# Wider weight conversion and a seven-product scheme for block 0's second product, with w_out's sums on VectorE

## The chip, the cores and the metric

The kernel runs on one core of a Trainium2 chip. The metric is device time in microseconds (us). "Span" is the time from the first to the last instruction of the profiled execution; it is some 2 us shorter than the time.

## The reference, cut to what matters

```python
for t in range(S):                       # B=4, H=8, S=768, D=64
    state = gamma * state + k[t] (outer) v[t]
    y[t] = scale * q[t] @ state
x = y as (3072 tokens, 512)
h = x @ w_in                             # 512 x 2048
g = h * sigmoid(1.702 * h)
out = g @ w_out                          # 2048 x 512
```

The weights come as 64-bit floats and are narrowed to 32-bit ones on the chip, with integer operations on the halves of each number.

## The kernel before

The tokens go in six blocks of 512 (m = 0 to 5), each of four chunks of 128 (24 chunks, j). Per chunk, `turn` transposes q and k, `attend` multiplies k and q and applies a mask, and `finish` gives x and the next state. Then come two products per block, "up" (x @ w_in, with a gate) and "down" (gated @ w_out). Blocks 2 to 5 use a seven-product scheme (Strassen-Winograd) for both; block 1 for the second; block 0 for none, since the sums of weight blocks that the scheme needs aren't there yet.

While TensorE does the plain up-products, VectorE and ScalarE convert the weights, one piece of 512 numbers per partition at a time:

```python
def narrow(n=1):
    ...
        act.activation(m, hi, AF.Abs, scale=2.0 ** 16)
        dve.tensor_scalar(m, m, MOST, LEAST, op0=min, op1=max)
        dve.tensor_scalar(mu, mu, 3, None, op0=logical_shift_left)
        dve.scalar_tensor_tensor(hi, hi, 0x80000000, mu, op0=and, op1=or)
        dve.tensor_scalar(mu, hi, 0xFF800000, None, op0=and)
        dve.scalar_tensor_tensor(r, lo, 2.0 ** -52, m, op0=mult, op1=mult)
        dve.tensor_add(w, hi_f, lo_f)
        fetch()                                    # the next piece
...
load(0); fetch(); load(1)                          # q, k, v of chunks 0 and 1
for _ in range(NRAW - 1): fetch()                  # NRAW = 4 pieces ahead
turn(0)                                            # issues chunk 2's q and k
for j in range(CB):                                # the head
    attend(j); narrow(1); turn(j + 1); finish(j); narrow(1)
    if j: up0(0, j - 1)
...
for f in range(NFF): up1(f); narrow(1)             # block 1's up-product
for f in range(NFF):                               # block 0's second product, 64 x 512 columns
    down0(f)
    if f % 4 == 3: sums_w2(f // 2 - 1)             # w_out's sums, on GpSimd
for m in range(1, NB): ...                         # blocks 1 to 5
```

Of the kernel before, what the change touches and what calls it, by code (L numbers as in the profile page):

```python
# [9 lines left out]
F32 = mybir.dt.float32  # L10
# [3 lines left out]
P = 128  # L14
# [14 lines left out]
def kernel(  # L29
# [64 lines left out]
    G0 = one.tile([P, 2, TH], F32, name="g0", tag="s1")  # L94
# [10 lines left out]
    def load(j, what="qkv"):  # L105
# [13 lines left out]
        else:  # L119
            for name, src in (("q", q), ("k", k)):  # L120
                t = two.tile([P, HP, P // C4, C4], F32, name=name + "_sq")
                for r0 in range(0, P, C4):
                    d0 = r0 % D
                    for hp in range(HP):
                        sp.dma_start(t[r0:r0 + C4, hp],
                                     src[b, 2 * hp + r0 // D, rows, d0:d0 + C4].rearrange("(s p) d -> p s d", p=C4))
                QKV[name, j] = t
            if c < NC - 1:
                plain("kn", k, "kn", 1)
        if "v" in what:  # L130
# [5 lines left out]
    NRAW = 4  # L136
    RAWS = [W2[:, 4 + i // 2, i % 2 * 4:i % 2 * 4 + 4].rearrange("p n e -> p (n e)").bitcast(U32)
            .rearrange("p (n two) -> p n two", two=2) for i in range(NRAW)]


    PIECES = []
    for p in range(NP):
        for h in range(2):
            dst = W1[:, p, 0:4:3] if h == 0 else W1[:, p, 1:3]
            PIECES.append((dst.rearrange("p ab c f -> p c ab f"), w1v[:, 2 * h:2 * h + 2, 2 * p * P:2 * (p + 1) * P],
                           dst.rearrange("p ab c f -> p ab (c f)")))
    for p in range(NP):
        for ab in range(2):
            dst = W2[:, 0:4:3, p] if ab == 0 else W2[:, 1:3, p]
            PIECES.append((dst, w2v[:, 2 * p + ab], dst))  # L150
    N1 = 2 * NP
    fetched = [0]

    def fetch():
        i = fetched[0]
        if i < len(PIECES):
            x = RAWS[i % NRAW]
            src = PIECES[i][1]
            sp.dma_start(x.rearrange("p (c f) two -> p c f two", c=2) if i < N1 else x, src)
            fetched[0] = i + 1  # L160
# [3 lines left out]
    def narrow(n=1):  # L164


        for _ in range(n):
            i = narrowed[0]
            if i == len(PIECES):
                return  # L170
            narrowed[0] = i + 1
            (w, _, m), x = PIECES[i], RAWS[i % NRAW]
            mu = m.bitcast(U32)
            two_runs = x.rearrange("p (a b) two -> p a b two", a=2)
            lo, hi = two_runs[:, :, :, 0], two_runs[:, :, :, 1]

            tc.keep_in_program_order(act.activation(m, hi.bitcast(F32), AF.Abs, scale=2.0 ** 16))
            tc.keep_in_program_order(dve.tensor_scalar(m, m, F64_MOST * 2.0 ** 16, F64_LEAST * 2.0 ** 16,  # L178
                                                       op0=ALU.min, op1=ALU.max))
            dve.tensor_scalar(mu, mu, 3, None, op0=ALU.logical_shift_left)  # L180
            dve.scalar_tensor_tensor(hi, hi, 0x80000000, mu, op0=ALU.bitwise_and, op1=ALU.bitwise_or)  # L181
            dve.tensor_scalar(mu, hi, 0xFF800000, None, op0=ALU.bitwise_and)  # L182
            r = lo.bitcast(F32)
            dve.scalar_tensor_tensor(r, lo, 2.0 ** -52, m, op0=ALU.mult, op1=ALU.mult)  # L184
            xf = x.bitcast(F32)
            if i < N1:
                xf = xf.rearrange("p (c ab f) two -> p c ab f two", c=2, ab=2)
                dve.tensor_add(w, xf[:, :, :, :, 1], xf[:, :, :, :, 0])
            else:
                xf = xf.rearrange("p (s e) two -> p s e two", s=2)  # L190
# [366 lines left out]
```

## Time and profile before

| | before |
|---|---|
| time, median of 4 | 732.94 us (732.53 to 735.52) |
| span of the profiled execution | 730.7 us |
| first up-product starts | 25.79 us |
| third up-product starts; from here TensorE isn't idle until 171.0 us | 46.99 us |
| block 1's up-product starts | 113.36 us |
| block 0's second product starts | 168.30 us |
| block 1's second product starts | 225.97 us |

The starts are read from TensorE's timeline. A line of a timeline gives the start and duration in us, the engine, the source line, the operation, output and inputs, the shape and the count, and in brackets how long the engine was idle before it and what ended that. The chain view gives start, duration and work only; its pieces start up to 0.17 us later than the timeline's, where two matmuls overlap. The lines of before are in the prediction.

### The profile page before, as it was taken

To read this page: it belongs to the slowest core of one execution; us is meant where nothing else is said; L and a number is where in the kernel's file an instruction comes from. 1 tells how busy PE (TensorE), PEld (TensorE's weight loads), DVE (VectorE), ACT (ScalarE), POOL (GpSimd) and SP (SyncE) were. 2 spreads that over 40 slices of the span, in tenths; PEclk is the share of its full clock that TensorE was granted. 3 is DMA by queue.
4 is the path that set the end of the run, shared out by engine and by line. 5 is a ranking of instruction groups with operands and counts; after the bars stand their busy time and mean duration, and the time that the engine had idled before them with its cause. 6 is when DMAs were issued, how large, how long until landed. Compare 5 with 4: busy or idle time off the path is not lost.

```text
span 730.7 us, 9512 instructions
## 1 busy us (share of the span) xinstructions
PE 710.6 (97%) x3680; PEld 569.1 (78%) x3680; DVE 365.0 (50%) x603; ACT 126.5 (17%) x209; POOL 137.9 (19%) x127
## 2 busy tenths in 40 slices
PE   5799999998999999999999999999999999999997
PEld 4678885443447888888888888888888888888886
DVE  4999977994002643442653344464344272244251
ACT  3322313330000000332000233000233000133000
POOL 3231010028533223000233100022200140200030
PEclk9999999999999999999999999999999999999999
DMA  9876454530001324300334310234300210100001
GB/s 244 212 179 172 119 125 100 157 123 1 0 0 59 73 47 85 71 1 1 66 56 89 61 21 1 49 57 88 74 10 0 49 39 1 44 1 0 15 0 44
DMA packets 142252, 46.26 MB, mean 63 GB/s; under 512 B 129920, under 2 KB 135552, under 8 KB 142208
## 3 DMA queue, kind: packets, MB, share of 16 engines
q1 hardware_dynamic: 135504, 39.10, 24.1%
q10 hardware_dynamic: 6704, 6.57, 2.7%
q8 instruction: 29, 0.48, 0.3%
q14 instruction: 15, 0.12, 0.1%
HBM read 39.33 MB, written 6.29 MB: 62 GB/s over the span
## 4 chain that ended last, share of the span: by engine, by line
PE 85%; DVE 13%; DMA 1%; issue 1%; SPq 0%; ACT 0%
PE pd L408 32%; PE px L357 15%; PE py L357 11%; PE po L317 7%; PE ph L292 7%; PE py L249 3%; PE pa L232 3%; PE pu L262 3%; PE py L245 2%; DVE W L184 2%; DVE W L181 2%; DVE W L191 1%; DVE G L279 1%; DVE W L178 1%; DVE W L182 1%; DMA q_in<-in_q_dram 1%
## 5 line engine op out<-in xcount | busy, mean ns | idle before, releaser
L408 PE MATMUL pd<-W,G 128*128 128x256 f32 x1120 | 250.3, 381 | 0.4 <-DVE G L348 0.3
L408 PEld LDWEIGHTS pd<-W,G 128*128 128x128 f32 x1120 | 210.1, 190 | 31.2 <-DVE G L348 1.2
L357 PE MATMUL px<-X,W 128*128 128x256 f32 x512 | 119.0, 379 | 0.0
L357 PEld LDWEIGHTS px<-X,W 128*128 128x128 f32 x512 | 97.3, 190 | 13.2
L357 PE MATMUL py<-X,W 128*128 128x256 f32 x384 | 90.7, 379 | 0.0
L357 PEld LDWEIGHTS py<-X,W 128*128 128x128 f32 x384 | 73.0, 190 | 9.9
L292 PE MATMUL ph<-X,W 128*128 128x256 f32 x256 | 58.2, 382 | 2.2 <-DVE X L253 2.2
L223 POOL TENSOR_TENSOR kd<-kn_in,cold 128x512 f32<-128x512 f32 x13 | 14.9, 1147 | 240.0 <-DMA q_sq<-in_q_dram 126.5
L305 PE MATMUL ph<-W,W 128*128 128x512 f32 x128 | 55.1, 592 | 0.0
L292 PEld LDWEIGHTS ph<-X,W 128*128 128x128 f32 x256 | 47.5, 190 | 8.9 <-DVE X L253 2.4
L349 POOL TENSOR_TENSOR G<-G 128x512 f32<-128x512 f32 x20 | 28.9, 1443 | 111.6 <-DVE G L348 107.0
L235 DVE TENSOR_TENSOR at<-pa,mask 128x512 f32<-128x512 f32 x32 | 20.6, 684 | 58.7 <-PE pa L232 58.7
L305 PEld LDWEIGHTS ph<-W,W 128*128 128x128 f32 x128 | 24.3, 190 | 30.2 <-issue 29.4
L317 PE MATMUL po<-W,W 128*128 128x512 f32 x96 | 42.8, 593 | 2.5 <-DVE G L279 2.5
L279 DVE TENSOR_TENSOR G<-G,sg 128x512 f32<-128x512 f32 x48 | 33.0, 688 | 13.8 <-ACT sg L277 13.8
L277 ACT ACTIVATE sg<-G 128x512 f32<-128x512 f32 x48 | 30.3, 631 | 51.0 <-DVE G L367 30.7
L317 PEld LDWEIGHTS po<-W,W 128*128 128x128 f32 x96 | 18.2, 190 | 25.8 <-issue 22.0
L277 ACT ACTIVATE sg<-ph 128x512 f32<-128x512 f32 x32 | 19.1, 598 | 105.0 <-PE ph L292 44.0
L269 POOL TENSOR_TENSOR state<-state,cold 64x256 f32<-64x256 f32 x32 | 23.2, 725 | 46.4 <-DVE state L267 23.1
L367 DVE TENSOR_TENSOR G<-py,p 128x512 f32<-128x512 f32 x16 | 11.1, 692 | 37.8 <-PE py L357 37.8
L320 DVE COPY o<-po 128x512 f32<-128x512 f32 x4 | 2.8, 692 | 51.8 <-PE po L317 50.3
L395 ACT ACTIVATE u<-pd 128x512 f32<-128x512 f32 x5 | 3.0, 597 | 134.1 <-PE pd L408 134.1
(87 smaller groups left out, 696.7 us busy)
## 6 DMA issues: line engine op xcount, KB each, us to landing
W<-in_moe_w_in_dram SPq DMA_DIRECT2D x16, 512.0 KB, 3.8
W<-in_moe_w_out_dram SPq DMA_DIRECT2D x16, 512.0 KB, 3.5
v_in<-in_v_dram SPq DMA_DIRECT2D x24, 256.0 KB, 4.0
out_dram<-o ACTq DMA_DIRECT2D x24, 256.0 KB, 2.3
kn_in<-in_k_dram SPq DMA_DIRECT2D x21, 256.0 KB, 3.6
q_sq<-in_q_dram SPq DMA_DIRECT2D x256, 16.0 KB, 1.9
k_sq<-in_k_dram SPq DMA_DIRECT2D x256, 16.0 KB, 1.8
q_in<-in_q_dram SPq DMA_DIRECT2D x8, 256.0 KB, 4.6
```

The source lines that it names most:

```text
L232: pe.matmul(p[:, i, hp, :], KT[j][r, hp, :], QT[j][r, hp, :], start=True, stop=True)
L249: pe.matmul(y[i * D:(i + 1) * D, hp, :], vn[:, 2 * hp + i, :], a[:, i, hp, :], start=(not c and hp == 0), stop=(hp == HP - 1), skip_group_ ...
L262: pe.matmul(u[:, hp, :], kd[:, h, :].rearrange("p i d -> p (i d)"), vn[:, h, :].rearrange("p i d -> p (i d)"), start=True, stop=True)
L269: pool.tensor_mul(new[r, :, r], old[r, :, r], cold[r, 2 * H:, None].to_broadcast([D, HP, D]))
L277: act.activation(s, h, AF.Sigmoid, scale=1.702)
L279: dve.tensor_mul(g, h[:, i], s[:, i])
L292: pe.matmul(h[:, ab], w, X[:, 2 * half + c // 2, c % 2, :], start=(ab == 0 and c == 0), stop=(c == 3), skip_group_check=True)
L305: pe.matmul(h, w, X1[:, c // 2:4:2, c % 2, :], start=(c == 0), stop=(c == 3))
L317: pe.matmul(PO[n], g0(p, 2 * half + ab)[:, t0:t0 + P], w, start=(f == 0), stop=(f == NFF - 1))
L349: pool.tensor_sub(g[1], g[1], g[0])
L357: pe.matmul(acc[:, u, :], W1[:, 2 * d + u, sa, c, :], X[:, sb, c, :], start=(start and u == 0 and c == 0), stop=(stop and c == 1), skip_gr ...
L408: pe.matmul(p0[:, n, :], G[:, p, sa, n * P:(n + 1) * P], W2[:, sb, p, :], start=(new and p == 0 and n == 0), stop=(last and p == NP - 1), ...
```

## The change

Four things change together. The weights are converted 1024 numbers at a time (all but the first two pieces), which makes half as many VectorE instructions of it. By 512 a tensor_scalar operation steps in 0.34 us and a two-input one in 0.60. There are six raw buffers instead of four, so six pieces are fetched ahead. Block 0's second product uses the seven-product scheme. For that w_out's sums must be ready before it, and they move from GpSimd to VectorE. A fifth thing goes with the first: the calls of the converter stand differently, so that by the program's order 22 of the 32 pieces come before block 1's up-product, where it was 18.

```diff
-    NRAW = 4
+    RAWS = [... for r in (W2[:, 4], W2[:, 5], G[:, 6:8]...)]    # three of 1024, six pieces
 def narrow():
+        n = 1 if i < 2 else 2
...
-    for _ in range(NRAW - 1):
+    for _ in range(5):
         fetch()
...
 for f in range(NFF):
     up1(f)
-    narrow(1)
+    if f % 2 == 0:
+        narrow()
+    if f >= NFF - 4:
+        sums_w2(2 * (f - NFF + 4))            # three sums each, now dve.tensor_sub
-for f in range(NFF):
-    down0(f)
-    if f % 4 == 3:
-        sums_w2(f // 2 - 1)
-for m in range(1, NB):
+for m in range(NB):
...
     for n, unit in enumerate(down(m)):
         unit()
+        if m == 0 and n < NP // 2:
+            sums_w2_t3(2 * n)                 # the fourth sum, dve.tensor_sub
```

(Cut: the operand numbering, where block 0's gated values are kept, and the converter's calls in the head and beside block 0's up-product. The loads of transposed q and k are now kept in program order.)

More of the change, by code (lines that the diff above doesn't have):

```diff
@@ L93 @@
     G = const.tile([P, NP, 4, TH], F32, name="G")
-    G0 = one.tile([P, 2, TH], F32, name="g0", tag="s1")
+    G0 = one.tile([P, 2, TH], F32, name="g0", tag="kd")
     X1 = W2[:, 6].rearrange("p (s c) t -> p s c t", s=4)
@@ L124, in load @@
                     for hp in range(HP):
-                        sp.dma_start(t[r0:r0 + C4, hp],
-                                     src[b, 2 * hp + r0 // D, rows, d0:d0 + C4].rearrange("(s p) d -> p s d", p=C4))
+                        tc.keep_in_program_order(sp.dma_start(
+                            t[r0:r0 + C4, hp],
+                            src[b, 2 * hp + r0 // D, rows, d0:d0 + C4].rearrange("(s p) d -> p s d", p=C4)))
                 QKV[name, j] = t
@@ L135 @@
     w2v = moe_w_out.bitcast(U32).rearrange("(f p) (e two) -> p f e two", p=P, two=2)
-    NRAW = 4
-    RAWS = [W2[:, 4 + i // 2, i % 2 * 4:i % 2 * 4 + 4].rearrange("p n e -> p (n e)").bitcast(U32)
-            .rearrange("p (n two) -> p n two", two=2) for i in range(NRAW)]
-    PIECES = []
-    for p in range(NP):
-        for h in range(2):
-            dst = W1[:, p, 0:4:3] if h == 0 else W1[:, p, 1:3]
-            PIECES.append((dst.rearrange("p ab c f -> p c ab f"), w1v[:, 2 * h:2 * h + 2, 2 * p * P:2 * (p + 1) * P],
-                           dst.rearrange("p ab c f -> p ab (c f)")))
@@ L147, with raw @@
-    for p in range(NP):
-        for ab in range(2):
-            dst = W2[:, 0:4:3, p] if ab == 0 else W2[:, 1:3, p]
-            PIECES.append((dst, w2v[:, 2 * p + ab], dst))
-    N1 = 2 * NP
+    RAWS = [r.rearrange("p a b -> p (a b)").bitcast(U32)
+            for r in (W2[:, 4], W2[:, 5], G[:, 6:8].rearrange("p a s t -> p a (s t)"))]
+    SRC = [w1v[:, 2 * h:2 * h + 2, 2 * p * P:2 * (p + 1) * P] for p in range(NP) for h in range(2)] \
+        + [w2v[:, f] for f in range(NFF)]
     fetched = [0]
+    def raw(i, n=1):
+        x = RAWS[i // 2 % 3]
+        return x[:, i % 2 * 1024:(i % 2 + n) * 1024]
@@ L154, in fetch @@
     def fetch():
         i = fetched[0]
-        if i < len(PIECES):
-            x = RAWS[i % NRAW]
-            src = PIECES[i][1]
-            sp.dma_start(x.rearrange("p (c f) two -> p c f two", c=2) if i < N1 else x, src)
+        if i < len(SRC):
+            x = raw(i).rearrange("p (n two) -> p n two", two=2)
+            sp.dma_start(x.rearrange("p (c f) two -> p c f two", c=2) if i < NFF else x, SRC[i])
             fetched[0] = i + 1
     narrowed = [0]
-    def narrow(n=1):
-        for _ in range(n):
-            i = narrowed[0]
-            if i == len(PIECES):
-                return
-            narrowed[0] = i + 1
-            (w, _, m), x = PIECES[i], RAWS[i % NRAW]
-            mu = m.bitcast(U32)
-            two_runs = x.rearrange("p (a b) two -> p a b two", a=2)
-            lo, hi = two_runs[:, :, :, 0], two_runs[:, :, :, 1]
-            tc.keep_in_program_order(act.activation(m, hi.bitcast(F32), AF.Abs, scale=2.0 ** 16))
-            tc.keep_in_program_order(dve.tensor_scalar(m, m, F64_MOST * 2.0 ** 16, F64_LEAST * 2.0 ** 16,
-                                                       op0=ALU.min, op1=ALU.max))
-            dve.tensor_scalar(mu, mu, 3, None, op0=ALU.logical_shift_left)
-            dve.scalar_tensor_tensor(hi, hi, 0x80000000, mu, op0=ALU.bitwise_and, op1=ALU.bitwise_or)
-            dve.tensor_scalar(mu, hi, 0xFF800000, None, op0=ALU.bitwise_and)
-            r = lo.bitcast(F32)
-            dve.scalar_tensor_tensor(r, lo, 2.0 ** -52, m, op0=ALU.mult, op1=ALU.mult)
-            xf = x.bitcast(F32)
-            if i < N1:
-                xf = xf.rearrange("p (c ab f) two -> p c ab f two", c=2, ab=2)
-                dve.tensor_add(w, xf[:, :, :, :, 1], xf[:, :, :, :, 0])
-            else:
-                xf = xf.rearrange("p (s e) two -> p s e two", s=2)
-                dve.tensor_add(w, xf[:, :, :, 1], xf[:, :, :, 0])
@@ new lines, in narrow @@
+    def narrow():
+        i = narrowed[0]
+        if i == len(SRC):
+            return
+        n = 1 if i < 2 else 2
+        narrowed[0] = i + n
+        p, h = i // 2 % NP, i % 2
+        if i < 2:
+            m = W1[:, 1, 2 * h:2 * h + 2].rearrange("p s c f -> p (s c f)")
+            w = W1[:, 0, h:4:2].rearrange("p ab c f -> p c ab f")
+        elif i < NFF:
+            m = W1[:, p, 0:4].rearrange("p s c f -> p (s c f)")
+            w = W1[:, p, 0:4].rearrange("p (ab h) c f -> p (h c) ab f", ab=2)
+        else:
+            m = w = W2[:, 0:4, p]
+        x = raw(i, n).rearrange("p (n two) -> p n two", two=2)
+        lo, hi = x[:, :, 0], x[:, :, 1]
+        if i >= NFF:
+            lo, hi = [t.rearrange("p (s e) -> p s e", s=4) for t in (lo, hi)]
+        mu = m.bitcast(U32)
+        tc.keep_in_program_order(act.activation(m, hi.bitcast(F32), AF.Abs, scale=2.0 ** 16))
+        tc.keep_in_program_order(dve.tensor_scalar(m, m, F64_MOST * 2.0 ** 16, F64_LEAST * 2.0 ** 16,
+                                                   op0=ALU.min, op1=ALU.max))
+        dve.tensor_scalar(mu, mu, 3, None, op0=ALU.logical_shift_left)
+        dve.scalar_tensor_tensor(hi, hi, 0x80000000, mu, op0=ALU.bitwise_and, op1=ALU.bitwise_or)
+        dve.tensor_scalar(mu, hi, 0xFF800000, None, op0=ALU.bitwise_and)
+        dve.scalar_tensor_tensor(lo.bitcast(F32), lo, 2.0 ** -52, m, op0=ALU.mult, op1=ALU.mult)
+        lo, hi = lo.bitcast(F32), hi.bitcast(F32)
+        if i < NFF:
+            lo, hi = [t.rearrange("p (c ab f) -> p c ab f", ab=2, f=P) for t in (lo, hi)]
+        dve.tensor_add(w, hi, lo)
+        for _ in range(n):
@@ L201, in home @@
         if j >= 2 * CB:
-            return one.tile([P] + shape, F32, name=name)
-        t = G[:, j % 2 * 4 + at, 0:2 if at < 3 else 4].rearrange("p s t -> p (s t)")
+            return one.tile([P] + shape, F32, name=name, tag=name)
         if at < 3:
-            return t.rearrange("p (a b) -> p a b", a=shape[0])
-        return t.rearrange("p (a b c) -> p a b c", a=2, b=HP)
+            t = G[:, at, j % 2 * 2:j % 2 * 2 + 2]
+            return t.rearrange("p s t -> p (s t)").rearrange("p (a b) -> p a b", a=shape[0])
+        return G[:, 3 + j % 2].rearrange("p s t -> p (s t)").rearrange("p (a b c) -> p a b c", a=2, b=HP)
     def turn(j):
@@ L218, in turn @@
             else:
-                dve.transpose(t.rearrange("p h t -> p (h t)"), QKV.pop((name, j)).rearrange("p h s d -> p (h s d)"))
+                tc.keep_in_program_order(dve.transpose(
+                    t.rearrange("p h t -> p (h t)"), QKV.pop((name, j)).rearrange("p h s d -> p (h s d)")))
             store[j] = t
@@ L279, in hidden, with g, g1 @@
             dve.tensor_mul(g, h[:, i], s[:, i])
-    def g0(p, s):
+    def g(m, p, s):
+        if m:
+            return G[:, p:p + 2, s, :]
         if s < 3:
-            return W1[:, p, 4 + s].rearrange("p c f -> p (c f)")
-        return X[:, 4 + p // 2, p % 2] if p < 6 else G0[:, p % 2]
+            return W1[:, p:p + 2, 4 + s].rearrange("p a c f -> p a (c f)")
+        return X[:, 4 + p // 2] if p < 6 else G0
+    def g1(m, p, s):
+        return g(m, p // 2 * 2, s)[:, p % 2]
     def up0(half, p):
@@ L290, in up0 @@
             for c in range(4):
-                w = W1[:, p, (c // 2 if ab == 0 else (3, 2)[c // 2]), c % 2, :]
+                w = W1[:, p, 2 * ab + c // 2, c % 2, :]
                 pe.matmul(h[:, ab], w, X[:, 2 * half + c // 2, c % 2, :], start=(ab == 0 and c == 0), stop=(c == 3),
@@ L296, in up0 @@
         else:
-            hidden([(g0(p, 2 + i), i) for i in range(2)], h)
+            hidden([(g1(0, p, 2 + i), i) for i in range(2)], h)
     def up1(f):
@@ L303, in up1 @@
         for c in range(4):
-            w = W1[:, p, (c // 2 if ab == 0 else (3, 2)[c // 2]), c % 2, :]
+            w = W1[:, p, 2 * ab + c // 2, c % 2, :]
             pe.matmul(h, w, X1[:, c // 2:4:2, c % 2, :], start=(c == 0), stop=(c == 3))
         hidden(G[:, p, ab:4:2, :], h)
-    PO = {}
-    def down0(f):
-        p, ab = divmod(f, 2)
-        for n in range(CB):
-            if f == 0:
-                PO[n] = ps.tile([P, 2, EH], F32, name="po", tag="xy"[n % 2])
-            half, t0 = divmod(n * P, TH)
-            w = W2[:, 0:4:3, p, :] if ab == 0 else W2[:, 1:3, p, :]
-            pe.matmul(PO[n], g0(p, 2 * half + ab)[:, t0:t0 + P], w, start=(f == 0), stop=(f == NFF - 1))
-            if f == NFF - 1:
-                o = two.tile([P, 2, EH], F32, name="o")
-                dve.tensor_copy(o, PO[n])
-                act.dma_start(out[n * P:(n + 1) * P, :], o.rearrange("p a e -> p (a e)"))
@@ L324, in sums_w1 @@
     def sums_w1(p):
         w = [W1[:, p:p + 2, s] for s in range(7)]
-        pool.tensor_add(w[4], w[3], w[2])
-        pool.tensor_sub(w[6], w[0], w[3])
+        pool.tensor_add(w[4], w[2], w[3])
+        pool.tensor_sub(w[6], w[0], w[2])
         pool.tensor_sub(w[5], w[4], w[0])
-        pool.tensor_sub(w[3], w[1], w[5])
-    def sums_b(b):
-        pool.tensor_sub(b[4], b[3], b[0])
-        pool.tensor_sub(b[6], b[2], b[3])
-        pool.tensor_sub(b[5], b[2], b[4])
-        pool.tensor_sub(b[3], b[1], b[5])
@@ L338, in sums_w2, with sums_x @@
-    def sums_w2(p):
-        sums_b([W2[:, s, p:p + 2, :] for s in range(7)])
-    def sums_x():
-        sums_b([X[:, s] for s in (0, 1, 3, 2, 4, 5, 6)])
-    def sums_g(p):
-        g = [G[:, p:p + 2, s, :] for s in range(4)]
-        dve.tensor_add(g[3], g[2], g[3])
-        dve.tensor_sub(g[2], g[0], g[2])
-        dve.tensor_sub(g[0], g[3], g[0])
-        pool.tensor_sub(g[1], g[1], g[0])
+        pool.tensor_sub(w[2], w[1], w[5])
+    def sums_x():
+        pool.tensor_sub(X[:, 4], X[:, 2], X[:, 0])
+        pool.tensor_sub(X[:, 6], X[:, 3], X[:, 2])
+        pool.tensor_sub(X[:, 5], X[:, 3], X[:, 4])
+        pool.tensor_sub(X[:, 2], X[:, 1], X[:, 5])
@@ new lines, in sums_w2, with sums_w2_t3, sums_g @@
+    def sums_w2(p):
+        w = [W2[:, s, p:p + 2, :] for s in range(7)]
+        dve.tensor_sub(w[4], w[1], w[0])
+        dve.tensor_sub(w[5], w[3], w[4])
+        dve.tensor_sub(w[1], w[2], w[5])
+    def sums_w2_t3(p):
+        dve.tensor_sub(W2[:, 6, p:p + 2, :], W2[:, 5, p:p + 2, :], W2[:, 0, p:p + 2, :])
+    def sums_g(m, p):
+        a = [g(m, p, s) for s in range(4)]
+        dve.tensor_add(a[3], a[2], a[3])
+        dve.tensor_sub(a[2], a[0], a[2])
+        dve.tensor_sub(a[0], a[3], a[0])
+        pool.tensor_sub(a[1], a[1], a[0])
@@ L358, in product @@
                               start=(start and u == 0 and c == 0), stop=(stop and c == 1), skip_group_check=True)
-        g = [G[:, 2 * d:2 * d + 2, s, :] for s in range(4)]
+        a = [G[:, 2 * d:2 * d + 2, s, :] for s in range(4)]
         x = ps.tile([P, 2, TH], F32, name="px", tag="x")
@@ L366, in up @@
         product(y, 1, 1, True, True)
-        dve.tensor_add(g[0], y, p1)
-        hidden(g[0], g[0])
+        dve.tensor_add(a[0], y, p1)
+        hidden(a[0], a[0])
         product(x, 5, 5, False, False)
@@ L379, in up @@
         y = ps.tile([P, 2, TH], F32, name="py3", tag="y")
-        product(y, 3, 3, True, True)
-        dve.tensor_add(g[3], z, vv)
-        hidden(g[3], g[3])
-        dve.tensor_add(g[2], y, t)
-        hidden(g[2], g[2])
-        product(x, 2, 2, False, True)
-        hidden(g[1], x)
+        product(y, 2, 3, True, True)
+        dve.tensor_add(a[3], z, vv)
+        hidden(a[3], a[3])
+        dve.tensor_add(a[2], y, t)
+        hidden(a[2], a[2])
+        product(x, 3, 2, False, True)
+        hidden(a[1], x)
     def down(m):
@@ L407, in part @@
                 for n in range(2):
-                    pe.matmul(p0[:, n, :], G[:, p, sa, n * P:(n + 1) * P], W2[:, sb, p, :],
+                    pe.matmul(p0[:, n, :], g1(m, p, sa)[:, n * P:(n + 1) * P], W2[:, sb, p, :],
                               start=(new and p == 0 and n == 0), stop=(last and p == NP - 1), skip_group_check=True)
@@ L422, in down @@
         P_ = [("x", 0, 0, True, False, lambda x: keep("p1", "s1", x)),
-              ("y0", 1, 1, True, True, lambda y: put(0, 0, y, kept["p1"])),
-              ("y1", 3, 3, True, True, lambda y: None),
+              ("y0", 1, 2, True, True, lambda y: put(0, 0, y, kept["p1"])),
+              ("y1", 3, 1, True, True, lambda y: None),
               ("x", 0, 5, False, False, lambda x: keep("u", "s2", x)),
@@ L427, in down @@
               ("x", 2, 6, False, True, then_p7),
-              ("x2", 1, 2, True, True, lambda y: put(0, 1, y, kept["t"]))]
+              ("x2", 1, 3, True, True, lambda y: put(0, 1, y, kept["t"]))]
         todo = []
@@ L434, in unit @@
                     if n == 2:
-                        sums_g(2 * d)
+                        sums_g(m, 2 * d)
                 todo.append(unit)
@@ L470 @@
     turn(0)
-    units = [(half, p) for p in range(3, NP) for half in range(2)]
     for j in range(CB):
         attend(j)
-        narrow(1)
+        narrow()
         turn(j + 1)
         finish(j)
-        narrow(1)
-        if j:
+        if j == 0:
+            narrow()
+        else:
             up0(0, j - 1)
     between = chunks(1)[1:]
-    for n, unit in enumerate([(1, p) for p in range(3)] + units):
+    for n, unit in enumerate([(1, p) for p in range(3)] + [(half, p) for p in range(3, NP) for half in range(2)]):
         up0(*unit)
-        if n < NP or n % 2:
-            narrow(1)
+        if n % 2 == 0:
+            narrow()
         if between:
@@ L488 @@
         up1(f)
-        narrow(1)
+        if f % 2 == 0:
+            narrow()
+        if f >= NFF - 4:
+            sums_w2(2 * (f - NFF + 4))
         if f >= NFF - 2:
             load(2 * CB + f - NFF + 2)
-    for f in range(NFF):
-        down0(f)
-        if f % 4 == 3:
-            sums_w2(f // 2 - 1)
-    for m in range(1, NB):
-        between = chunks(m + 1) if m + 1 < NB else []
+    for m in range(NB):
+        between = chunks(m + 1) if 0 < m < NB - 1 else []
         if m > 1:
```

## The prediction

Three passages of the prediction are cut: on VectorE beside GpSimd, on what an instruction costs, and on the rates of two kinds of operation. This case shows only the times beside them. No term of the sum is cut: 732.8 - 8.6 - 0.5 + 0.4 = 724.1 us. The 0.07 us fixed is the author's estimate from the steps of 0.34 and 0.60 us, and the closing 0.34 and 0.60 are the steps of a tensor_scalar and of a two-input operation of 512 numbers. The 10 us of slack in rival 2 is an estimate as well: three buffers beyond the one in use, at 54.8/16 = 3.43 us each.

> **What bounds the kernel now.** I read the page's engine rows first, then the chain that ended last, then that chain in order of time, and last the timelines of the places where the chain leaves TensorE. From the page:
>
> ```profile
> PE 710.6 (97%) x3680; PEld 569.1 (78%) x3680; DVE 365.0 (50%) x603; ACT 126.5 (17%) x209; POOL 137.9 (19%) x127
> PE   5799999998999999999999999999999999999997
> PEld 4678885443447888888888888888888888888886
> DVE  4999977994002643442653344464344272244251
> PE 85%; DVE 13%; DMA 1%; issue 1%; SPq 0%; ACT 0%
> ```
>
> The reader is to see two things. TensorE is busy in every slice after the second, so nearly everything that leaves its stream comes off the time, and nothing else does. VectorE is full only in the first quarter, while the weights are converted. The 13% that the chain gives to VectorE look like a second bound, but TensorE is busy all that while: the chain merely follows one wait back through the converter. The chain in order of time and TensorE's timeline around that wait:
>
> ```profile
> 113.53 3.45 PE ph L305 x8
> ...
> 171.21 1.63 DVE W L191
> 173.50 52.62 PE po L317 x122
> 226.13 6.91 PE pd L408 x32
> ```
> ```profile
> 159.71 8.75 PE L305 MATMUL ph<-W,W 128*128 128x512 f32 x20
> 168.30 2.74 PE L317 MATMUL po<-W,W 128*128 128x512 f32 x6
> 173.50 2.84 PE L317 MATMUL po<-W,W 128*128 128x512 f32 x6 [2.47 <-DVE G L279]
> ```
>
> These give the rates. A 512-wide matmul record takes 52.62/122 = 0.4313 us, a 256-wide one 6.91/32 = 0.2159 us: the same per column, so narrow products cost nothing extra. (The mean durations in the group rows, 593 and 381 ns, overlap and mustn't be added.) The program's matmuls each make two records: 64 of block 0's second product give 96 + 24 + 8 = 128. That product runs from 168.30 to 226.13, 57.83 us: 128 x 0.4313 = 55.21, plus the wait of 2.47.
>
> That wait is the converter's tail, on VectorE's timeline:
>
> ```profile
> 156.36 0.41 DVE L182 TENSOR_SCALAR W<-W 128x512 uint32<-128x512 uint32 x1
> 156.69 0.41 DVE L178 TENSOR_SCALAR W<-W 128x512 f32<-128x512 f32 x1
> 157.03 0.67 DVE L184 SCALAR_TENSOR_TENSOR W<-W 128x512 f32<-128x512 uint32 x1
> ...
> 169.54 1.64 DVE L184 SCALAR_TENSOR_TENSOR W<-W 128x512 f32<-128x512 uint32 x1
> 171.21 1.63 DVE L191 TENSOR_TENSOR W<-W 128x512 f32<-128x512 f32 x1
> 172.77 0.68 DVE L279 TENSOR_TENSOR G<-ph,sg 128x512 f32<-128x512 f32 x1
> ```
>
> VectorE runs back to back, and where GpSimd has begun w_out's sums a 0.68 us operation takes 1.64. The last block-0/1 gate (the multiply at 172.77) is late, it holds a PSUM buffer, and the product starts late.
>
> [...] 0.68 becomes 1.64 beside GpSimd. [...] a 256-wide multiply in a run of independent ones steps in 0.34 us (54.73 to 55.07), a 512-wide one in 0.60, so 0.26 is streaming and about 0.07 fixed. [...] the trace's steps are 0.34 and 0.60.
>
> **The change, part by part.**
> Block 0's product. Removed: 128 records of 512 = 55.21 us, and the wait of 2.47. Added: 7 products x 4 units x 4 matmuls = 112, or 224 records of 256, x 0.2159 = 48.36 us. Exactly seven eighths. This lies wholly on TensorE, on the path. The new product starts on gates finished long before (block 0's) and needs one PSUM buffer that the third-last gate frees, so I take the 2.47 as gone. It brings the wait that every seven-product block has between its third and fourth product, where the operand sums are made. The last block, which like block 0 has no attention work beside it, shows its size:
>
> ```profile
> 677.00 26.41 PE L408 MATMUL pd<-W,G 128*128 128x256 f32 x120
> ...
> 695.03 1.58 POOL L349 TENSOR_TENSOR G<-G 128x512 f32<-128x512 f32 x1 [67.37 <-DVE G L348]
> 695.52 1.64 DVE L347 TENSOR_TENSOR G<-G 128x512 f32<-128x512 f32 x1
> ...
> 703.69 22.71 PE L408 MATMUL pd<-W,G 128*128 128x256 f32 x104 [0.28 <-DVE G L348]
> ```
>
> 120 x 0.2159 = 25.91, so TensorE restarts 703.69 - 677.00 - 25.91 = 0.8 us late. Stage after: 48.36 + 0.8 = 49.2; before 57.8; gain **8.6 us**.
>
> Conversion by 1024. One piece of 512 is three tensor_scalar and three two-input operations: 3 x 0.34 + 3 x 0.60 = 2.8 us where independent work fills the gaps, 3.43 where each waits for the one before (118.24 to 121.67). A pair of 1024, by the fixed 0.07, is 3 x 0.60 + 3 x 1.13 = 5.2, or 5.8 with those waits once instead of twice. Saved per pair 0.4 to 1.05; 15 pairs, 6.5 to 15.8 us of VectorE. Most of it lies beside a full TensorE: from 47 to 168 us TensorE never stops, so it's worth nothing there except as room.
>
> What takes the room: w_out's sums, 12 + 4 two-input operations x 0.60 to 0.73 = 10 to 12 us, from GpSimd (16 operations, some 22 us) to VectorE. In the first product's second half (113.5 to 168.3) VectorE was busy 52.1 of 54.8. Now ten pieces are left there at most on plan, five pairs: 5 x 5.8 + 16 gates x 0.65 + 12 sums x 0.65 = 47 us. It fits, with GpSimd out of the way, and the last sums aren't needed until the third product, 14 us later.
>
> The head (0 to 47 us). This is the one place where a faster converter could shorten the path. TensorE's timeline:
>
> ```profile
> 18.46 0.63 PE L216 MATMUL pt<-ident,q_in 128*128 128x128 f32 x4 [1.32 <-DMA q_in<-in_q_dram]
> ...
> 25.79 3.72 PE L292 MATMUL ph<-X,W 128*128 128x256 f32 x16 [2.17 <-DVE X L253]
> ...
> 36.20 3.62 PE L292 MATMUL ph<-X,W 128*128 128x256 f32 x16
> ...
> 46.99 3.19 PE L292 MATMUL ph<-X,W 128*128 128x256 f32 x14
> ```
>
> Between 25.79 and 46.99 its idle gaps add up to 0.96 + 1.45 = 2.4 us; that's all that two faster cycles can win. Before 25.79 the first two pieces stay at 512 and win nothing, and two more weight pieces are now fetched ahead of chunk 2's q and k: 1.05 MB at the 241 GB/s that 10 to 26 us show is 4.3 us. Those q would land near 22.8 instead of 18.46. VectorE has the second pair to do meanwhile, so not all is lost, but I expect the first up-product at some 27.7 (+1.9). Net for the head: +1.9 - 2.4 = -0.5.
>
> Everything else moves names only: x's and w_in's sums stay on GpSimd with the same count, and blocks 1 to 5 keep their products. I add 0.4 us for longer VectorE operations that hold up an attention mask or a gate now and then. Sum: 732.8 - 8.6 - 0.5 + 0.4 = **724.1 us**, 1.2% less.
>
> **The rivals.**
> (1) The head decides. If VectorE bounds it alone, three pairs save 3 us there and the total is about 721.5; the near-full VectorE speaks for it, the DMA share of 1.00 from 10 to 26 us against it. If instead the later q and coarser operations let TensorE wait in each cycle, the head loses 3 to 4 us: 727.5.
> (2) VectorE becomes the bound in 90 to 168 us: six w_out pieces rather than two are converted before the second half, and the 12 sums follow. If gates come late behind 1.13 us operations, TensorE waits for PSUM and gains vanish: some 729. Against it: VectorE sat idle about 9 us between 90 and 120, and four PSUM buffers give 10 us of slack.
> (3) The operand sums of block 0 stall more than the last block's: their operands lie in three tensors, and four of w_out's sums run just before. With two such waits of 2 us, 727.
> (4) The seven-product gain is hidden by something else in that stage. I find nothing: DMA's share there is 0.01, VectorE's busy time 6.5 of 57.8.
>
> **Range and chances.** The 8.6 is firm to about 1 us. Head and frictions can each move 3 us either way, so 720.0 to 728.5 should hold it 8 times in 10. A gain over 2% needs less than 718.1: the head would have to give 6 us more than I see: 0.05. Slower by over 2%, above 747.4, needs a new bound all through the first 170 us: 0.01. Within 2%: 0.94.
>
> **What would show it.** Right: in the profile after, block 0's second product has 224 records at 0.216 us, takes 49 to 50 us and starts without a wait; in the fourth product's start a wait near 0.8 us on VectorE's operand sums; the second half of the first product still takes 55.2 us for 128 records; VectorE has idle time before its last gates; 1024-wide tensor_scalar steps are 0.60 us and two-input ones 1.13; the first up-product starts near 27.7 and the third near 46.5; from block 1 on nothing has changed but its start, some 8.7 us earlier. Wrong: a wait of several us of a TensorE row of the first stages on VectorE, or a first up-product after 30 us.

## The result

The changed kernel takes 725.18 us (median of 4, 724.48 to 726.33) against 732.94. The ratio is 0.9888, with a 95% interval of 0.9861 to 0.9916. Ratios here are the mean time of one kernel's fast runs over that of the other's in the same rounds, so they aren't quite the ratio of the medians quoted. That is within 2%, 7.8 us less, and 1.1 us over the prediction.

From the page of the profile after: the busy row, TensorE by slices, VectorE by slices, the granted TensorE clock by slices, and the chain's shares by engine.

```profile
PE 705.4 (98%) x3776; PEld 588.5 (81%) x3776; DVE 373.2 (52%) x542; ACT 126.7 (18%) x197; POOL 125.7 (17%) x115
PE   5799999999999999999999999999999999999997
DVE  4888889993612822443743353553345373244251
PEclk9899999999999999999999999999999999999999
PE 92%; DVE 5%; DMA 1%; ACT 1%; issue 0%; SPq 0%; ACTq 0%
```

The dip that TensorE had in its tenth slice, the wait at 173.50, is gone. In its place the clock has an 8 in the second slice, where before every slice had a 9. TensorE's timeline, around block 0's second product (now line 403):

```profile
114.10 55.10 PE L313 MATMUL ph<-W,W 128*128 128x512 f32 x128
169.03 13.98 PE L403 MATMUL pd<-W,W 128*128 128x256 f32 x64
...
195.73 1.99 PE L403 MATMUL pd<-W,W 128*128 128x256 f32 x8 [0.28 <-DVE W L343]
```

The product follows without a gap, and the one wait in it is the one at the operand sums. In the head:

```profile
21.57 1.09 PE L217 MATMUL pt<-ident,q_in 128*128 128x128 f32 x4 [4.41 <-DMA q_in<-in_q_dram]
...
24.25 2.08 PE L247 MATMUL py<-G,state 128*128 128x128 f32 x8 [0.46 <-ACT G L218]
26.25 1.97 PE L251 MATMUL py<-G,v_in 128*64 128x128 f32 x16
28.15 1.16 PE L264 MATMUL pu<-v_in,G 128*128 128x128 f32 x8
29.32 3.72 PE L300 MATMUL ph<-X,W 128*128 128x256 f32 x16
...
47.73 7.07 PE L300 MATMUL ph<-X,W 128*128 128x256 f32 x32
```

Chunk 2's q comes 3.1 us later than before, and then TensorE is slow: the four transposes take 1.09 us where before they took 0.63. The view by stretches of time shows why. Its columns are the stretch, its length, busy time and instructions of PE, PEld, DVE, ACT and POOL, then the granted clock, the DMA share and GB/s:

```profile
16.00:21.50 5.50, 1.17 (x17) 0.97 (x16) 5.32 (x11) 0.00 (x0) 2.04 (x2) 0.98 1.16 322
21.50:25.00 3.50, 2.93 (x11) 2.18 (x12) 2.89 (x5) 2.43 (x4) 1.41 (x1) 0.50 1.20 278
```

The clock falls to half near the end of the idle time; in steps of 0.25 us the view has it at 0.50 from 21.3 to 28.1 us. So here an idle time of 4.41 us goes with a clock of 0.50; in runs below it fell with less (3.16 and 2.86 us). ScalarE's timeline shows a second delay in the same place: its copies of chunk 2's q and k (line 218) stand behind the second pair's first step, which waits for the first pieces' scratch: the magnitudes of the first two pieces are worked out in the place of the second pair, so the second pair's first step waits for them. It shows as the 0.46 us that TensorE waits at 24.25. VectorE's timeline, the second below, has a third limit: chunk 1's X, which the first up-product needs, stands behind five of the second pair's six steps.

```profile
22.55 1.17 ACT L181 ACTIVATE W<-W 128x1024 f32<-128x1024 f32 x1 [7.21 <-DVE W L187]
23.62 1.04 ACT L218 ACTIVATE G<-pt 128x512 f32<-128x512 f32 x2
```
```profile
27.44 1.23 DVE L187 SCALAR_TENSOR_TENSOR W<-W,W 128x1024 f32<-128x1024 uint32 x1
28.58 0.68 DVE L255 TENSOR_TENSOR X<-py,rowd 128x512 f32<-128x512 f32 x1
```

X is done at 29.26 and TensorE at 29.31 (28.15 + 1.16), so the two limits arrive together, and the first up-product starts at once.

Stage by stage, from the starts on TensorE's timelines:

| stage | before | after | difference |
|---|---|---|---|
| to the first up-product | 25.79 | 29.32 | +3.53 |
| first to third up-product | 21.20 | 18.41 | -2.79 |
| to block 1's up-product | 66.37 | 66.37 | 0.00 |
| block 1's up-product | 54.94 | 54.93 | -0.01 |
| block 0's second product, with waits | 57.67 | 49.25 | -8.42 |
| the rest | 504.73 | 504.22 | -0.51 |
| span | 730.7 | 722.5 | -8.2 |

The last -0.5 lies after the last matmul: 4.3 us before and 3.8 after, in writing out the last output; its cause wasn't looked for.

### The profile page after: what moved, and what is told of

Read it like the earlier page. It is cut to its first block, busy times and chain, and to the rows that moved or that the text cites. A ratio compares the mean times of both kernels' runs of the same rounds, so it can differ in the third digit from the quotient of the medians.

```text
span 722.5 us, 9662 instructions
## 1 busy us (share of the span) xinstructions
PE 705.4 (98%) x3776; PEld 588.5 (81%) x3776; DVE 373.2 (52%) x542; ACT 126.7 (18%) x197; POOL 125.7 (17%) x115
## 4 chain that ended last, share of the span: by engine, by line
PE 92%; DVE 5%; DMA 1%; ACT 1%; issue 0%; SPq 0%; ACTq 0%
PE pd L403 38%; PE px L352 15%; PE py L352 11%; PE ph L313 8%; PE ph L300 7%; PE py L251 3%; PE pa L234 3%; PE pu L264 3%; PE py L247 2%; DMA q_in<-in_q_dram 1%; PE pt L217 1%; DVE W L342 1%; DVE G L342 1%; DVE W L343 1%; DVE G L343 1%; ACT W L181 0%
## 5 line engine op out<-in xcount | busy, mean ns | idle before, releaser
L279 ACT ACTIVATE sg<-G 128x512 f32<-128x512 f32 x48 | 30.3, 630 | 50.9 <-DVE G L362 30.6
L403 PE MATMUL pd<-W,W 128*128 128x256 f32 x160 | 35.6, 380 | 0.4 <-DVE W L343 0.3
L403 PEld LDWEIGHTS pd<-W,W 128*128 128x128 f32 x160 | 30.2, 190 | 5.6 <-DVE W L343 1.2
L271 POOL TENSOR_TENSOR state<-state,cold 64x256 f32<-64x256 f32 x32 | 25.6, 800 | 44.0 <-DVE state L269 24.8
L255 DVE TENSOR_TENSOR X<-py,rowd 128x512 f32<-128x512 f32 x20 | 13.8, 688 | 33.3 <-PE py L251 33.3
```

Source lines behind the costliest of these rows:

```text
L271: pool.tensor_mul(new[r, :, r], old[r, :, r], cold[r, 2 * H:, None].to_broadcast([D, HP, D]))
L279: act.activation(s, h, AF.Sigmoid, scale=1.702)
L403: pe.matmul(p0[:, n, :], g1(m, p, sa)[:, n * P:(n + 1) * P], W2[:, sb, p, :], start=(new and p == 0 and n == 0), stop=(last and p == NP - ...
```

## The experiments

My theory after the result: the product and the wait before it give the 8.4 us; the larger conversion gives something between the first and the third up-product; and the two extra pieces fetched ahead of chunk 2's q give part of it back (theory A). The rival for the head (theory B) is VectorE's order: in the built program the second pair stood ahead of chunk 1's X, so the first up-product might have been late with any q.

### The head: fetch order, VectorE's order, and the clock

**Four pieces ahead.**

```diff
-    for _ in range(5):
+    for _ in range(3):
         fetch()
...
     turn(0)
+    for _ in range(2):
+        fetch()
```

> The changed kernel, with four weight pieces instead of six fetched ahead of chunk 2's q and k (the other two right behind them). In the changed kernel q of chunk 2 lands at 21.57 us, TensorE has then been idle for 4.41 us, its granted clock is 0.50 from 21.5 to 25 us, and the first up-product starts at 29.32 (before: 25.79). Theory A (the two extra pieces ahead of q delay it, and the idle time lowers TensorE's clock besides): q lands near 18.5 us again, the clock stays at 1.00, the first up-product starts at 25 to 26.5 us, and some 2 to 3 us of this reach the end: 722 to 723.5 us. Theory B (VectorE decides: the first pair of 1024 stands ahead of chunk 1's X): q lands early, but the first up-product stays within 1 us of 29.3 and the time at 725.

Measured: 722.67 us (722.01 to 724.71), ratio 0.985. TensorE's timeline:

```profile
18.68 0.63 PE L217 MATMUL pt<-ident,q_in 128*128 128x128 f32 x4 [0.71 <-DMA q_in<-in_q_dram]
...
24.91 3.72 PE L300 MATMUL ph<-X,W 128*128 128x256 f32 x16 [0.94 <-DVE X L255]
...
45.39 4.91 PE L300 MATMUL ph<-X,W 128*128 128x256 f32 x22
```

The q is there at 18.68 us, the clock is 1.00, and the first up-product starts 4.4 us earlier. Of this 2.3 us are left at the third up-product (45.39 against 47.73), and the same 2.3 at the end (span 720.2 against 722.5): the rest is lost to gaps while VectorE catches up. This is what theory A foretold. One reservation: with the loads in this order the built program also puts chunk 1's X ahead of the second pair on VectorE, so this run doesn't exclude B.

**VectorE's order alone.** The second pair is converted after chunk 1 is finished.

```diff
         attend(j)
-        narrow()
+        if j != 1:
+            narrow()
         turn(j + 1)
         finish(j)
-        if j == 0:
+        if j < 2:
             narrow()
-        else:
+        if j:
             up0(0, j - 1)
```

> The changed kernel, with the first pair of 1024 converted after chunk 1 is finished, so that VectorE writes chunk 1's X before it; the fetches as in the changed kernel. Theory A (q's late arrival and the halved clock): the half-speed TensorE work ends at 28.2 us all the same, the first up-product starts at 28.8 to 29.3, under 0.6 us are won: 725 us. Theory B (VectorE's order): X is written as soon as TensorE is done, and if VectorE was what held it, the first up-product starts 1.5 us or more earlier, with a time near 723.

Measured: 726.71 us (726.03 to 726.83), ratio 0.9898. The first up-product starts at 27.38 us, 1.9 us earlier, where theory A allowed under 0.6. So A alone isn't enough. But the 1.9 us aren't the order's alone either: q comes 0.37 us earlier in this execution, ScalarE's wait of 0.46 is gone, and TensorE's clock is back at 25.7 us instead of 28.1. X then waits for TensorE, where in the changed kernel the two were ready together. The order is a limit of its own all the same: in the run with the sums on GpSimd, below, whose clock was back at 27.2, TensorE waits 0.69 us for X. The time isn't shorter (both theories had 725 or less), since the third up-product comes at 49.26: the next chunk's mask now stands behind the pair, with waits of 1.24 and 1.30 us. This order moves the delay, and doesn't remove it.

**Both.** The two edits above together.

> Both: four pieces ahead of chunk 2's q, and the first pair converted after chunk 1 is finished. Theory A: within 0.7 us of the run with four pieces alone, in the first up-product (25 to 26.5 us) and in the time (722 to 723.5). Theory B: at least 1.5 us under the run with four pieces alone.

Measured: 722.96 us (722.74 to 723.32), first up-product at 24.77. Equal to four pieces alone, as A says. But in both runs X stands ahead of the pair, so their equality doesn't test B. That the early loads shorten the time is shown; how much of it is q's arrival and how much the order of VectorE's work that comes with it is not.

**The clock, first try.**

```diff
         narrow()
+        if j == 1:
+            spare = ps.tile([P, HP, P], F32, name="spare", tag="x")
+            for r in range(28):
+                pe.transpose(spare[:, r % HP, :], ident, ident)
         turn(j + 1)
```

> The changed kernel, with 28 idle transposes of the identity put on TensorE while it waits for chunk 2's q, results not used. They take nothing away from the wait for q, but leave TensorE no idle time of 4.4 us. Theory A with the clock as its second part: the granted clock stays at 1.00 after 21.5 us, the two chunk-2 transposes take 0.63 us instead of 1.09 and the eight state products 1.16 instead of 2.08, and the first up-product starts at 27.3 to 28 instead of 29.32; at most 1.5 us reach the end: 723.7 to 725. Without a part of the clock: first up-product at 29.3 or later, time 725 to 726.

Measured: 725.99 us (724.37 to 726.05), first up-product at 30.88. Inconclusive. The transposes ran at full speed, 0.60 us, but then TensorE waited 3.16 us for ScalarE, which was behind the pair's first step, and the clock fell after all (0.73 from 25 to 30 us). It needed the other order to be a test.

**The clock, second try.** 36 idle transposes in the kernel with the pair converted late.

> The run with the first pair converted late, with 36 idle transposes on TensorE while it waits for chunk 2's q (so that ScalarE's copies of chunk 2's q and k are not held behind the pair's first step, as they were in the first run with idle transposes). The clock as a cause: the granted clock stays at 1.00 from 16 to 30 us, chunk 2's transposes take 0.63 us instead of 1.09 and the state products 1.1 instead of 1.92, and the first up-product starts 0.8 to 1.6 us before the 27.38 of the run without them. If the clock was of no consequence: within 0.4 us of 27.38. The time isn't a test here: the later masks are what held that run.

Measured: one look, 726.54 us; first up-product at 27.01. TensorE's timelines, first of the run with the late pair, then with idle transposes added:

```profile
21.20 1.09 PE L217 MATMUL pt<-ident,q_in 128*128 128x128 f32 x4 [5.32 <-DMA q_in<-in_q_dram]
...
27.38 3.62 PE L300 MATMUL ph<-X,W 128*128 128x256 f32 x16
```
```profile
18.57 4.15 PE L473 MATMUL spare<-ident 128*128 128x128 f32 x36
22.55 0.60 PE L217 MATMUL pt<-ident,q_in 128*128 128x128 f32 x4
...
27.01 3.62 PE L300 MATMUL ph<-X,W 128*128 128x256 f32 x16
```

I had put in too many: they end at 22.6, after q had come, so the start moved by only 0.37 us, which by my own numbers would say "of no consequence". The stretch from chunk 2's transposes to the first up-product says more: 27.38 - 21.20 = 6.18 us at half clock and 27.01 - 22.55 = 4.46 at full, so the halved clock costs 1.7 us there. That reading was chosen after the run, and rests on one execution.

**The changed kernel again**, on the chip of the last comparison:

> The changed kernel itself, beside the run with both edits on the same chip, as the other reference: 724.5 to 726 us, some 4 us over the run with both edits if the two edits add up, 3 or less if part is given back.

Measured: 725.27 us (724.03 to 726.64), ratio 0.9888. Its profiled execution is a slower one than the first, and shows how this head varies. Chunk 0's state update, at 15.10 us, takes 2.08 us, where it took 1.16 in the first profile; the first pieces are late, and ScalarE's copies behind them come so late that TensorE waits 2.72 us:

```profile
26.21 2.08 PE L247 MATMUL py<-G,state 128*128 128x128 f32 x8 [2.72 <-ACT G L218]
...
31.57 3.62 PE L300 MATMUL ph<-X,W 128*128 128x256 f32 x16
```

The first up-product starts at 31.57 instead of 29.32, and the span is 2.2 us longer (724.7). The clock fell in an idle time of 2.86 us and stayed at 0.50 for 10.2 us, from 20.9 to 31.1. In the first profile it was 6.8 us, and 3.4 us in the first run with idle transposes; these different lengths may make up part of the spread. (The view gives 1.00 until the clock first changes, also at 4.5 us, where the first transposes take 1.09 us: there go by the durations.) So the head of a single execution of this kernel is uncertain by some 2 us, and a difference of that size can't be read from one profile.

### The product, its sums and the conversion

**The old product.** Block 0's second product as before, with the rest changed.

```diff
-        if f >= NFF - 4:
-            sums_w2(2 * (f - NFF + 4))
...
+    for f in range(NFF):
+        down0(f)
+        if f % 4 == 3:
+            sums_w2(f // 2 - 1)
+            sums_w2_t3(f // 2 - 1)
-    for m in range(NB):
+    for m in range(1, NB):
```

> The changed kernel with block 0's second product as before (64 matmuls of 512 columns), w_out's sums on VectorE after every fourth of its steps. My theory: the product takes 55.2 us instead of 48.4, with no wait of 0.8 in it, and starts with a wait of 0 to 2.5 us (of 2.47 before), since VectorE has time left at the end of the first product: 731 to 732.5, so that nearly all of the gain is gone. Rival: the gain came from the conversion and the wait: under 729.

Measured: 730.64 us (729.23 to 731.53), ratio 0.9962. The chain in order of time:

```profile
114.33 54.93 PE ph L313 x128
169.26 54.93 PE po L325 x128
224.20 6.91 PE pd L418 x32
```

The product takes 54.93 us with no wait before it, so the scheme itself gives 54.93 - 49.25 = 5.7 us of stage time and 5.4 us of time. The wait of 2.47 goes even with the old product, which my theory allowed for (0 to 2.5 us). The time is 0.4 us under the expected 731 to 732.5, and well over the rival's 729.

**The sums on GpSimd.**

```diff
-        dve.tensor_sub(w[4], w[1], w[0])      # and the other three
+        pool.tensor_sub(w[4], w[1], w[0])
```

> The changed kernel with w_out's sums on GpSimd again, all 16 operations. My theory: the sums' engine doesn't set the time, since the first of them is needed 14 us after block 0's second product starts and the conversions end 14 us before it: 12 operations of 1.3 to 1.6 us begin near 155 us and end near 173, the last four by 180, while the third product starts at 183; VectorE's last gates run beside GpSimd with some at 1.6 us and still come in time: 724.7 to 726. Rival: [...] the sums or gates come late, and TensorE waits: 727 or more.

Measured: 725.84 us (724.60 to 726.61), ratio 0.9902: the engine of the sums doesn't matter here. The product starts without a wait, and the span is 722.8. In one point the expectation was wrong. I had some gates at 1.6 us beside GpSimd. VectorE's and GpSimd's timelines:

```profile
163.26 0.69 DVE L281 TENSOR_TENSOR G<-ph,sg 128x512 f32<-128x512 f32 x1 [2.74 <-ACT sg L279]
```
```profile
163.34 2.49 POOL L332 TENSOR_TENSOR W<-W 128x512 f32<-128x512 f32 x2
```

The gate keeps its 0.69 us, and so do the other four that run beside GpSimd (156.39 to 170.13 us). Why, no run shows. In the kernel before, it was the converter's own operations that became 1.6 us (1.64 at 169.54 and 1.63 at 171.21, beside GpSimd), while the gates there kept 0.67 to 0.68.

**The conversion by 512.** One piece per call, two calls where the changed kernel has one; buffers, sums and product as changed.

```diff
-        n = 1 if i < 2 else 2
+        n = 1
...
         if n % 2 == 0:
             narrow()
+            narrow()
...
```

> The changed kernel (six pieces fetched ahead, seven-product block 0, w_out's sums on VectorE) with the weights converted 512 at a time, two calls where the changed kernel has one. My theory: the larger conversion is worth something only in the head, where VectorE does the work of three pairs before TensorE is full; 15 pairs cost VectorE some 13 us more, but beside a TensorE that is busy. First up-product within 1 us of 29.3 us, the third 1 to 3 us later than 47.73, then 55 us of the first product's second half unchanged: 726 to 728.5. Rival: VectorE becomes the bound before block 0's second product, with w_out's sums late behind the conversions: 730 or more. Other rival: the larger conversion is worth nothing anywhere: 725.

Measured: 727.09 us (726.28 to 727.95), ratio 0.9916; third up-product at 51.19; block 1's up-product 54.93 us; no wait before block 0's second product. The time, 1.9 us longer, is within the expectation; the first and third up-product, expected by 30.3 and 50.7, are later. The head was of the slow kind (first up-product at 31.68), and by the uncertainty above the profile doesn't show how much of it is the conversion. From the first to the third up-product, where the clock is back, it takes 19.51 us against 18.41. So it was run again below, with q in time.

**The wait at the operand sums.** The fourth operand sum, needed only by the seventh product, goes to VectorE after the fifth product, in block 0 and in the last block.

```diff
-        pool.tensor_sub(a[1], a[1], a[0])
+        if 0 < m < NB - 1:
+            pool.tensor_sub(a[1], a[1], a[0])
...
+                    if n == 4 and m in (0, NB - 1):
+                        tc.keep_in_program_order(dve.tensor_sub(g(m, 2 * d, 1), g(m, 2 * d, 1), g(m, 2 * d, 0)))
```

> The changed kernel with the last operand sum of block 0 and of the last block (a1 - a0, four operations each, needed only by the seventh product) on VectorE after the fifth product's units instead of on GpSimd beside the other sums. My theory: the wait of 0.8 us ahead of the fourth product's last unit comes from VectorE operations of 1.64 us beside GpSimd (0.69 alone), three of them per block; without GpSimd the three sums take 2.0 us for each 1.73 us of product and are ready in time, so both waits go: 1.6 us less, 723.2 to 724.2. Rival: the chain of dependent sums is itself too long, and the wait stays at 0.5 us or more in each: 724.6 to 725.5.

Measured: 722.74 us (722.31 to 723.82), ratio 0.9858. TensorE's and VectorE's timelines in the last block:

```profile
668.42 48.51 PE L404 MATMUL pd<-W,G 128*128 128x256 f32 x224
```
```profile
689.00 0.69 DVE L342 TENSOR_TENSOR G<-G 128x512 f32<-128x512 f32 x1
```

All 224 records are in one run, and the operation that took 1.64 us beside GpSimd takes 0.69. Both waits are gone; the span is 1.7 us shorter. The median is 2.4 us shorter, more than the expected 1.6; part of it is thus the head's spread.

**Both edits that gained**: four pieces ahead, and the fourth sum on VectorE.

> The changed kernel with four pieces ahead of chunk 2's q and the last operand sum of block 0 and of the last block on VectorE after the fifth product: the two single edits that shortened it. My theory: they act at different places (head 2.3 us, two waits of 0.8 us), so they add up: third up-product near 45.4 us, no wait inside block 0's and the last block's product, span 718.5 to 719, time 720.3 to 721.8, ratio to before 0.982 to 0.984. Rival: a TensorE that runs earlier meets VectorE or a transfer not yet done, and part is given back: 722 or more.

Measured: 720.44 us (719.36 to 721.58), ratio 0.9824, with a 95% interval of 0.98 to 0.9847; span 718.1; third up-product at 45.04. It is 12.7 us faster than the kernel before and 4.8 us faster than the changed one of the same rounds. The two add up.

**Both edits, by 512.**

> The run with both edits (four pieces ahead of chunk 2's q, last operand sum on VectorE), with the weights converted 512 at a time. The earlier run with 512 had chunk 2's q late and a head that differs by 2 us from execution to execution; here q comes in time and the clock stays up. My theory: the larger conversion saves VectorE some 3 us before the third up-product and nothing later, and TensorE's gaps there (2.2 us with both edits) show that part of it reaches the path: third up-product at 46 to 48 us instead of 45.04, the first product's second half 54.9 us, no wait before block 0's second product, time 721.5 to 723.5, ratio to before 0.984 to 0.987. Rival (the larger conversion is worth nothing once q is early): 719.8 to 721.2. Rival (512 leaves VectorE behind at the end of the first product, and block 0's second product waits): over 724.

Measured: 723.76 us (721.37 to 723.97), ratio 0.9859, against 0.9824 by 1024: (0.9859 - 0.9824) x 733 = 2.6 us. TensorE's timeline:

```profile
45.59 1.80 PE L254 MATMUL py<-G,v_in 128*64 128x128 f32 x14 [0.77 <-DVE G L240]
47.32 2.06 PE L267 MATMUL pu<-v_in,G 128*128 128x128 f32 x8
49.19 7.09 PE L303 MATMUL ph<-X,W 128*128 128x256 f32 x32
```

The median is 0.3 us over the expected range, and under the rival's 724. The 2.6 us are uncertain by about as much: the two intervals, 0.9837 to 0.9881 and 0.98 to 0.9847, overlap. Both pairs of runs point the same way, so the larger conversion gains some 2 us, by the profiles all of it in the head. The profiled execution, at 49.19 us, is outside the 46 to 48 expected for the third up-product. After waits of 0.83 and 0.77 us for the masks the clock had fallen there once more (0.50 from 45.8 to 49.2 us; 2.06 us for work that takes 1.16), and the execution is one of the slower three of five. From there on nothing differs: block 1's up-product takes 54.93 us, and block 0's second product follows without a wait.

## Why the prediction was right

**The product (8.6 us predicted, 8.4 measured).** The working held to the record: 224 records, seven eighths of the columns, one wait at the operand sums. In the reasons, one step was too narrow. I put the 2.47 us of wait down as gone because the new product starts on old gates and needs one buffer. The run with the old product has no wait either. VectorE ends the conversions at 155.6 us instead of 172.8, with GpSimd idle beside it. The run with the sums on GpSimd and the run by 512 have no wait either, so none of these three parts is needed to remove it. What no run undid are the six buffers and the order of the converter's calls. The traces have 17 of the 32 pieces done when block 1's up-product starts before, 20 after, and 19 in the run by 512. That is the likeliest cause, but not shown. So the scheme gives 5.7 us, and the rest of the change the 2.5.

**Room on VectorE: right.** VectorE was busy 50.97 us of block 1's up-product (47 predicted, with five pairs left; it was six), its last sums fit, and block 1's up-product took 54.93 us. Rival 2 fell, and so did rival 3: the wait at the operand sums was 0.8 us. That the sums moved to VectorE was worth nothing measurable: 725.84 with them on GpSimd.

**The head (-0.5 predicted, +0.7 in the first profile): the step that failed.** The term was "the first up-product at some 27.7 (+1.9)": q would be 4.3 us late, and 2.4 of these would be made good, since VectorE had the second pair to do meanwhile. Nothing was made good. q was 3.1 us late (21.57, where I had 22.8), and the first up-product 3.5 us late (29.32). From the one to the other I had allowed 4.9 us, and it took 7.75. Two things that the prediction left out stood there. TensorE ran at half clock until 28.1 us and was busy nearly all the time; in the second try, one execution, the halved clock was worth 1.7 us. And ScalarE's copies and chunk 1's X stood behind the second pair, so that X was ready no sooner than TensorE. The two overlap, so their shares can't be added, and no run separates them. The gain back, 2.4 predicted, was 2.8. Rival 1's second form had TensorE wait in each cycle, which it did no more than before (0.31 us); but its size, a loss of 3 us, is what the second profile of this kernel shows (third up-product at 49.87, +2.9).

**Frictions (+0.4 predicted): none.** From the third up-product to block 0's second product both kernels take 121.3 us.

Sum: -8.4, +0.7, 0 and -0.5 at the output's end give -8.2 in span, and 7.8 us less in time, where -8.7 was predicted. Part of this closeness is luck: the head was 1.2 us worse than predicted, and the missing frictions and the output's end took 0.9 back. What stays open is which part of the change removed the wait of 2.47, since each of the three undone alone leaves it away, and how the head's delay divides between the clock and the order of work.

## What to carry to other kernels

When one engine is full, price a change by that engine's records and waits, and look at a stage that has the same neighbours for the waits that the new form brings. Deeper prefetch isn't free: what is fetched ahead stands in front of the next thing needed (here chunk 2's q came at 21.57 us instead of 18.46), and an idle gap that it opens in TensorE can cost more than its own length: here, after 4.41 us idle, the clock stayed at 0.50 until 28.1 us, and the second try puts such a stretch at 1.7 us, in one execution. A cheap sum put on a "free" engine can slow the engine that matters (here a VectorE operation took 1.64 us beside GpSimd and 0.69 without); look at when its result is needed, and put it there.

## What else the traces show

- What waiting for the instruction before adds to a VectorE instruction's start: here a two-input operation of 512 numbers steps in 0.60 us among independent ones and in 0.72 to 0.74 when it waits for its predecessor: its whole 0.69 and 0.03 to 0.05 more.
- The order in which a build places an engine's work can move with a change of DMA order: here four pieces instead of six ahead also moved chunk 1's X in front of the second pair on VectorE. The first up-product came at 24.91 instead of 29.32 us; q's earlier arrival has a share in that.
- The fall of TensorE's clock to 0.50 goes with no one length of idle time here: it came with 4.41 us in the first profile, after 3.16 us in the first run with idle transposes, in an idle time of 2.86 us in the second profile of the changed kernel, and after several waits of under 1 us in the last run by 512.
